# A fused attention and two-MoE kernel: a new order of the first chunks, and the first eight units' second token halves run later, from raw weights

## The chip, the cores and the metric

The kernel runs on one core of one Trainium2 chip. The metric is the device time of one execution in microseconds (us). TensorE (PE), VectorE (DVE), ScalarE (ACT) and GpSimd (POOL) each execute their own instructions in program order; SyncE (SP) issues nearly all DMAs, in order too.

## The reference

Three stages follow each other, in float32.

```python
# attention: 4 batches x 8 heads, 768 tokens, head size 48; per token t
S = (ar + i*ai)/|a| * min(|a|, 0.999) * S + k_t v_t^T     # complex state, decay normalised
y_t = q_t . Re(S)
# MoE 1: 3072 tokens, 384 wide, 4 experts of 1024, dense
out = sum_e p_e * (relu(x @ w1[e]) @ w2[e]),   p = probs / sum(probs)
# MoE 2: 384 -> 2048 -> 384
h = x @ w_in;  out = maximum(0.01 * h, h) @ w_out
```

## The kernel before, in words

**Attention** is cut into 24 chunks of 128 tokens. `elementwise(c)` (L167 to L251) turns one chunk's inputs (`aaqk`, one 768 KB load) into features `ft` by some thirty operations on DVE, ACT and POOL: logarithms and exponentials of the decay, two prefix scans (L202, L207), a phase scan (L219), sine and cosine, and last the products with q and k (L243). `by_head(c)` copies `ft` by six SBUF to SBUF DMAs into `hd`, a layout by head (L261). `products(c)` is TensorE work: `pt` transposes (L279), scores `sc` (L292), the state `pm`/`st`, the output `py`, its transposes `px` (L325), from which ACT and DVE make `xh` and `xl` (L333, L334), the high and low part of the next stage's input.

**MoE 1 and MoE 2** run in units of 128 hidden columns: 32 units for MoE 1 (`u` 0 to 31), 16 for MoE 2, over six groups `g` of 512 tokens. Each product of two float32 numbers is made from high and low parts by three matmuls. A whole unit is `gemm_in` (nine matmuls into `ph`, L442), `hp` on DVE (L447), its split into `hh` on ACT and `hl` on DVE (L459, L460), and `gemm_out` (nine matmuls into `acc`, L471 to L473). In group 0 a weight comes raw from HBM (384 KB, L402), is split by an ACT cast and a POOL subtraction (`split_unit`, L418, L419) and stored as a high and low pair (768 KB, L608); later uses reload that pair (L410). Four raw buffers and seven split buffers are used in turn (`RAWS`, `WTS`).

**The order** is written out by hand. The list `order` (L379) names the units: the first eight units on tokens 0 to 255, the same eight on tokens 256 to 511 (with reloaded pairs), then units 8 to 31 whole. The main loop (L591) runs two units ahead with `gemm_in`. The attention of the first four chunks is partly run before the loop, by the string `PLAN`: each digit runs `elementwise` of that chunk up to its next `yield`, `p`, `q`, `r`, `t` do the same for `products` of chunks 0 to 3, `s` splits one weight half, `n` normalises the probabilities. The rest of the attention is `background()` (L516): its `yield`s are ticks, run between the halves of units at the speed that `pace` gives, so that each group's chunks are done before its units. Within a chunk's 26 ticks, `PSTEPS` says which belong to `products(c)`; the others run `elementwise(c + 1)`. The inputs of chunk c+2 are loaded at the start of chunk c's ticks (L532), ahead of `by_head(c)` in SP's queue. `warm` (L161) puts matmuls without use into TensorE's queue early on.

Of the kernel before, what the change touches and what calls it, by code (L numbers as in the profile page):

```python
# [11 lines left out]
F32 = mybir.dt.float32  # L12
# [8 lines left out]
P = 128  # L21
NT = B * S
DM = H * D
# [11 lines left out]
NHALF = 8  # L35
WARM = 1, 2, 3, 0
# [4 lines left out]
FTK = (1,)  # L41
TPOOL = 6
# [5 lines left out]
DEC = 33.0  # L48
PSTEPS = (1, 3, 5, 8, 10, 13, 16, 18, 21)
ESTEPS = 16  # L50
NSTEPS = ESTEPS + len(PSTEPS)
WAIT = 4
HDG = (1,)
AR_MAX = 1e4
# [7 lines left out]
def fused_kernel(  # L62
# [20 lines left out]
    with ExitStack() as fast:  # L83
# [25 lines left out]
        ones = const.tile([P, P], F32, name="ones")  # L109
        G.memset(ones, 1.0)  # L110
        zero_b = const.tile([P, 1], F32, name="zero_b")
        G.memset(zero_b, 0.0)
# [47 lines left out]

        def warm(x, n):  # L161

            out = ps_acc.tile([P, TG], F32, name="warm", tag="acc0")
            for _ in range(n):
                PE.matmul(out[:, : NG * P], ident, x.rearrange("p g t -> p (g t)"), start=True, stop=True)

        def elementwise(c):  # L167
# [14 lines left out]
            table("natural_log_exp_and_others")  # L182
            act(r, g, AF.Ln)
            act(a, g, AF.Square)
            T = V if c < TPOOL else G
            S = G if c < 2 else T
            S.tensor_tensor(b, en, en, ALU.mult)
            yield
            T.tensor_tensor(a, a, b, ALU.add)
            act(r, r, AF.Exp, scale=-1.0)  # L190
# [4 lines left out]
            act(a, a, AF.Ln)  # L195
            S.tensor_tensor(r, en, r, ALU.mult)
            yield
            act(b, a, AF.Exp, scale=-0.5, bias=ln_b)
            yield
# [8 lines left out]
            G.tensor_tensor(q, q, en, ALU.mult)  # L208
            act(a, b, AF.Exp, scale=-0.5)
            yield  # L210
            table("trig_and_small")
            act(r, r, AF.Arctan)
            V.scalar_tensor_tensor(b, en, -1.0, a, ALU.mult, ALU.mult)
            V.scalar_tensor_tensor(a, b, 2.0, a, ALU.add, ALU.mult)
# [5 lines left out]
            if c >= CPG:  # L220
                yield
# [3 lines left out]
            if c >= CPG:  # L225
                yield
# [11 lines left out]
            act(cs[:, 0], g, AF.Sin, scale=-1.0, bias=pi_b)  # L238
            if c == 1:
                warm(th, WARM[1])  # L240
            yield
            for i, x in ((0, q), (1, k)):
                (G if i and c in FTK else V).tensor_tensor(  # L243
                    ft[:, :, :, i * P : (i + 1) * P], cs,
                    x[:, None].to_broadcast([P, 2, NG, P]), ALU.mult,
                )
                if i or c >= CPG:
                    yield
            feats[c] = (ft, vt)
# [18 lines left out]
        def products(c):  # L268
# [7 lines left out]
            for ri in range(2):  # L276
# [7 lines left out]
                yield  # L284
            if c < 2:
                warm(last_phase[c], WARM[2])
            att = pool.tile([P, H, P], F32, name="att", bufs=1)
            for hh in range(2):
# [58 lines left out]
        stored = []  # L347

        def decode(i):
            u, half = divmod(i, 2)  # L350
# [16 lines left out]
            A.copy(wt[:, 0], wo)  # L367
            G.tensor_tensor(wt[:, 1], wo, wt[:, 0].bitcast(F32), ALU.subtract)
            yield
            load_raw64(i + 3)  # L370
            if stored:
                SP.dma_start(*stored.pop())
            stored.append((ws[NU1 + u][:, half], wt.bitcast(F32)))

# [16 lines left out]
        raws, wts, pbs, hs, x2 = {}, {}, {}, {}, {}  # L391
        seen = set()
        fresh = [u not in seen and not seen.add(u) and u < NU1 for _, u, _ in order]

# [17 lines left out]
        def split_unit(s, part):  # L412
            if s >= len(order) or not fresh[s]:
                return
            if s not in wts:
                wts[s] = p_w.tile([P, 2, 2, DM], F32R, name="wt", bufs=WTS)
            raw, wt = raws[s][:, part], wts[s][:, part]
            A.copy(wt[:, 0], raw)  # L418
            G.tensor_tensor(wt[:, 1], raw, wt[:, 0].bitcast(F32), ALU.subtract)  # L419
            if part:  # L420
                del raws[s]

        def load_pb(s):
            if s >= len(order) or order[s][1] >= NU1 or order[s][1] % 8 or order[s][2][0]:
                return
            g, e = order[s][0], order[s][1] // 8
            pb = p_h.tile([P, TG], F32, name="pb", bufs=2)
            SP.dma_start(pb, pn_d[e : e + 1, g * TG : (g + 1) * TG].to_broadcast([P, TG]))
            pbs[g, e] = pb
# [33 lines left out]
        def gemm_out(s, acc):  # L463
            u, (t0, t1) = order[s][1:]
            first, last = u in (0, NU1) and t0 == 0, u in ends
            wt = wts.pop(s)[:, 1]
            hh, hl = hs.pop(s)
            for dc in range(NG):
                cols = slice(dc * P, (dc + 1) * P)
                out = acc[dc][:, t0:t1]  # L470
                PE.matmul(out, wt[:, 0, cols], hh, start=first, stop=False)  # L471
                PE.matmul(out, wt[:, 1, cols], hh, start=False, stop=False)  # L472
                PE.matmul(out, wt[:, 0, cols], hl, start=False, stop=last)  # L473

# [14 lines left out]
        with tc.manual_schedule():  # L489
# [12 lines left out]
            steps.update(zip("pqrt", (products(c) for c in range(CPG))))  # L502
            splits = iter([(0, 0), (0, 1), (1, 0), (1, 1), (2, 0), (2, 1), (3, 0)])
            for x in PLAN + "0" * 14 + "1" * 14 + "pq" * 8 + "s" * 7:
                if x in steps:
                    next(steps[x], None)
                elif x == "n":
                    normalise_probs()
                    load_pb(0)
                elif x == "s":  # L510
                    for s, part in islice(splits, 1):
                        split_unit(s, part)
                        if part and s < 2:
                            load_unit(s + 5)

            def background():  # L516
                for _ in zipped(steps["2"], steps["3"]):
                    yield
# [26 lines left out]
            def decoding():  # L545
# [5 lines left out]
                yield  # L551
                SP.dma_start(*stored.pop())

            dec = decoding()

            first = max(0, 14 - min(PLAN.count("2"), PLAN.count("3"))) + WAIT + E2 - PLAN.count("r") - PLAN.count("t")
            pace = [(0.0, 0), (KN, first)]
# [33 lines left out]
            for s in range(len(order)):  # L591
# [233 lines left out]
```

## Time and profile before

| | before |
|---|---|
| median of three runs | 1506.38 us (1501.48, 1506.38, 2019.27) |
| profiled execution | 1506.07 us, of which its span 1504.2 us |
| TensorE busy | 1403.8 us, 93% of the span |
| VectorE / ScalarE / GpSimd busy | 57% / 38% / 18% |

A window row gives, for a stretch of the span, each engine's busy time, the granted TensorE clock as a share of 2.4 GHz, and the DMA engines' share and rate. A waits row gives what an engine's line waited for: total, times, longest. A timeline row begins with start and duration and ends with the idle time before it and what ended that, in brackets. "SPq" and "ACTq" are DMAs by the queue that issued them.

### The profile page before, as it was taken

The page shows a single profiled execution, that of the slowest core. Times are in us where ns is not written, and L with a number is a line of the kernel's source. Part 1 is how long each engine was busy: PE and PEld are TensorE (multiplying, and loading weights), DVE is VectorE, ACT ScalarE, POOL GpSimd, SP SyncE. Part 2 cuts the span into 40 slices and gives each one's busy share as a digit, 9 for nine tenths or more (in the row PEclk, how much of TensorE's full clock was granted, in tenths as well). Part 3 has the DMA queues.
Part 4 walks back from the last instruction along what each step waited for, and adds up shares of the span by engine and source line. Part 5 has one row for each costly group of instructions (what it writes and reads, how often), then busy time and mean ns, then how long its engine had stood idle before and what let it go on. Part 6 is the DMA issues. An engine that isn't in the chain of part 4 may idle for free.

```text
span 1504.2 us, 18506 instructions
## 1 busy us (share of the span) xinstructions
PE 1403.8 (93%) x6972; PEld 1177.8 (78%) x6972; DVE 864.8 (57%) x1503; ACT 566.7 (38%) x957; POOL 263.6 (18%) x251
## 2 busy tenths in 40 slices
PE   1888888999899989999999999999999999999997
PEld 0787667888777878878888888888888888888886
DVE  8838566669787878876455555455443333333332
ACT  5535455533444344355333354333242111323232
POOL 5113455311223122121001021001010000100000
PEclk9789989999999999999999999999999999999999
DMA  5498776887788698776776575676565655556562
GB/s 194 53 321 262 243 224 210 246 290 241 236 271 259 248 286 254 264 243 192 236 226 195 195 229 170 232 226 171 178 200 175 218 202 204 193 189 210 190 210 65
DMA packets 91042, 325.48 MB, mean 216 GB/s; under 512 B 10464, under 2 KB 32064, under 8 KB 90944
## 3 DMA queue, kind: packets, MB, share of 16 engines
q1 hardware_dynamic: 88064, 319.24, 66.8%
q10 hardware_dynamic: 2880, 4.98, 1.0%
q8 instruction: 56, 0.92, 0.3%
q14 instruction: 42, 0.34, 0.1%
HBM read 262.72 MB, written 42.52 MB: 203 GB/s over the span
## 4 chain that ended last, share of the span: by engine, by line
PE 60%; DVE 8%; DMA 3%; ACT 2%; issue 2%; POOL 0%; SPq 0%; DVEq 0%; ACTq 0%; POOLq 0%
PE ph L442 27%; PE acc L471 9%; PE acc L473 9%; PE acc L472 9%; DVE hl L460 2%; PE sc L292 1%; PE py L315 1%; PE py L317 1%; DMA vt<-in_v_dram 1%; DVE hp L447 1%; ACT hh L459 1%; DMA ws_scratch<-dw 1%; PE pm L303 1%; DVE ft L243 1%; DMA r<-in_w_dram 1%
## 5 line engine op out<-in xcount | busy, mean ns | idle before, releaser
L442 PE MATMUL ph<-xh,wt 128*128 128x512 f32 (+1 forms) x1200 | 407.5, 396 | 6.9 <-DMA wt<-ws_scratch 6.3
L471 PE MATMUL acc<-hh,wt 128*128 128x512 f32 (+1 forms) x888 | 350.0, 394 | 6.9 <-ACT o L586 6.9
L473 PE MATMUL acc<-hl,wt 128*128 128x512 f32 (+1 forms) x888 | 341.9, 385 | 0.0
L472 PE MATMUL acc<-hh,wt 128*128 128x512 f32 (+1 forms) x888 | 341.2, 384 | 0.0
L459 ACT CAST hh<-hp 128x512 fp32r<-128x512 f32 (+1 forms) x296 | 180.6, 610 | 402.1 <-DVE hp L447 315.4
L460 DVE TENSOR_TENSOR hl<-hp,hh 128x512 fp32r<-128x512 f32 (+1 forms) x296 | 213.5, 721 | 183.6 <-ACT hh L459 183.1
L442 PEld LDWEIGHTS ph<-xh,wt 128*128 128x128 f32 x1200 | 231.4, 195 | 51.8 <-DMA wt<-ws_scratch 7.4
L447 DVE SCALAR_TENSOR_TENSOR hp<-ph,pb 128x512 f32<-128x512 f32 (+1 forms) x200 | 133.4, 667 | 199.9 <-PE ph L442 199.8
L442 PE MATMUL ph<-xl,wt 128*128 128x512 f32 (+1 forms) x600 | 234.5, 391 | 1.1 <-DVE xl L334 1.1
L442 PE MATMUL ph<-x2h,wt 128*128 128x512 f32 x576 | 198.0, 398 | 0.0
L471 PEld LDWEIGHTS acc<-hh,wt 128*128 128x128 f32 x888 | 167.5, 189 | 38.2 <-ACT o L586 7.6
L473 PEld LDWEIGHTS acc<-hl,wt 128*128 128x128 f32 x888 | 167.1, 188 | 34.1
L472 PEld LDWEIGHTS acc<-hh,wt 128*128 128x128 f32 x888 | 167.7, 189 | 31.0
L450 DVE SCALAR_TENSOR_TENSOR hp<-hp 128x512 f32<-128x512 f32 x96 | 72.3, 753 | 171.7 <-ACT hp L449 171.7
L442 PEld LDWEIGHTS ph<-xl,wt 128*128 128x128 f32 x600 | 117.4, 196 | 22.0 <-DVE xl L334 1.6
L442 PEld LDWEIGHTS ph<-x2h,wt 128*128 128x128 f32 x576 | 108.7, 189 | 25.2
L449 ACT COPY hp<-ph 128x512 f32<-128x512 f32 x96 | 56.3, 586 | 168.0 <-PE ph L442 168.0
L442 PE MATMUL ph<-x2l,wt 128*128 128x512 f32 x288 | 114.5, 397 | 0.0
L292 PE MATMUL sc<-hd 96*128 96x128 f32 x384 | 58.3, 302 | 35.8 <-DMA hd<-ft 26.7
L292 PEld LDWEIGHTS sc<-hd 96*128 96x128 f32 x384 | 55.7, 215 | 42.8 <-issue 22.7
L419 POOL TENSOR_TENSOR wt<-raw,wt 128x384 fp32r<-128x384 f32 x64 | 71.9, 1144 | 57.2 <-ACT wt L418 56.9
L208 POOL TENSOR_TENSOR aaqk<-aaqk,ge 128x384 f32<-128x384 f32 x24 | 26.5, 1103 | 252.1 <-DVE ge L207 252.1
(94 smaller groups left out, 1467.2 us busy)
## 6 DMA issues: line engine op xcount, KB each, us to landing
wt<-ws_scratch SPq DMA_DIRECT2D x264, 768.0 KB, 4.8
ws_scratch<-wt SPq DMA_DIRECT2D x32, 768.0 KB, 8.1
hd<-ft SPq DMA_DIRECT2D x142, 128.5 KB, 7.2
aaqk<-in_attn_dram SPq DMA_DIRECT2D x22, 768.0 KB, 5.8
raw<-in_w_dram SPq DMA_DIRECT2D x32, 384.0 KB, 4.1
r<-in_w_dram SPq DMA_DIRECT2D x32, 384.0 KB, 3.8
ws_scratch<-dw SPq DMA_DIRECT2D x32, 384.0 KB, 4.2
pb<-pn_scratch SPq DMA_DIRECT2D x24, 256.0 KB, 6.5
```

Source lines behind the costliest of these rows:

```text
L208: G.tensor_tensor(q, q, en, ALU.mult)
L292: PE.matmul(sc[:, j], hd[:, h, P : 2 * P], hd[:, h, :P], start=True, stop=True)
L419: G.tensor_tensor(wt[:, 1], raw, wt[:, 0].bitcast(F32), ALU.subtract)
L442: PE.matmul(ph[:, : t1 - t0], wt[:, wi, cols], x[kc][:, t0:t1], start=n == 0, stop=n == 3 * NG - 1)
L447: V.scalar_tensor_tensor(hp, ph, 0.0, pbs[g, u // 8][:, t0:t1], ALU.max, ALU.mult)
L449: A.copy(hp, ph)
L450: V.scalar_tensor_tensor(hp, hp, 0.01, hp, ALU.mult, ALU.max)
L459: A.copy(hh, hp)
L460: V.tensor_tensor(hl, hp, hh.bitcast(F32), ALU.subtract)
L471: PE.matmul(out, wt[:, 0, cols], hh, start=first, stop=False)
L472: PE.matmul(out, wt[:, 1, cols], hh, start=False, stop=False)
L473: PE.matmul(out, wt[:, 0, cols], hl, start=False, stop=last)
```

## The change

Four things are done.

1. **Units of group 0.** After the first eight halves come units 8 to 15 whole, then, alternating, a whole unit (16 to 23) and a second half (0 to 7), then 24 to 31. Second halves load the raw weight again and split it again; the pair is stored only at that second time, and the eight reloads are gone. Unit 8's `gemm_out` runs in two column halves.
2. **Before the loop.** `warm` is gone. `PLAN` runs chunks 0 and 1 first and gives chunks 2 and 3 fewer steps; what is left of them runs in the ticks. Six weight halves are cast on ACT (`cast_early`), their low part is made by TensorE (identity times raw minus identity times high) and copied by ACT (`rest_early`), instead of by POOL. Chunks 0 and 1 issue three of their six `hd` DMAs each from ACT. Within `elementwise`, `Square` stands before `Ln`, and more `yield`s cut it finer; `ft` with k of chunk 1 is on DVE, not on POOL.
3. **Ticks.** Three more steps of `elementwise(c + 1)` stand between `by_head(c)` (step 1) and the scores (step 12 in place of 8), and `load_chunk(c + 2)` moves to step 9, behind `by_head`.
4. **Decoding of MoE 2's weights.** A store is issued one part later, and the next raw load after a `yield`.

The core of the diff:

```diff
-PLAN = "0100100111100n10s1s0s100s1s0s00110s22113p2q1332p322q32p2p3q2p3q3q2q3p23pq2pq223333"
+PLAN = (
+    "0101001010101011" "01ss0000mm" "00sss11mm000" "1111ppsm23111qq"
+    "23232n3pp23p2ppqq3q23qqpq23m"
+)
-PSTEPS = (1, 3, 5, 8, 10, 13, 16, 18, 21)
-ESTEPS = 16
+PSTEPS = (1, 3, 5, 12, 14, 17, 20, 22, 24)
+ESTEPS = 17
+LOADSTEP = 9
...
-                (G if i and c in FTK else V).tensor_tensor(
+                V.tensor_tensor(
...
-                    (A if c in HDG and i == ri else SP).dma_start(hd[row : row + DG], ft[:, ri, i])
+                    (A if c < 2 and (i == ri or i == 2 - ri) else SP).dma_start(hd[row : row + DG], ft[:, ri, i])
...
-        order = [(0, u, half) for half in halves for u in range(NHALF)] + first_stage(0)[NHALF:]
+        order = [(0, u, halves[0]) for u in range(NHALF)] + first_stage(0)[NHALF : 2 * NHALF]
+        for u in range(NHALF):
+            order += [(0, 2 * NHALF + u, whole), (0, u, halves[1])]
+        order += first_stage(0)[3 * NHALF :]
...
-        fresh = [u not in seen and not seen.add(u) and u < NU1 for _, u, _ in order]
+        fresh = [g == 0 and u < NU1 for g, u, _ in order]
...
+        def cast_early(s, part):
...
+            A.copy(wts[s][:, part, 0], raws[s][:, part])
+            early_cast.append((s, part))
+
+        def rest_early():
...
+            rest = ps_h.tile([P, TG], F32, name="ph")[:, :DM]
+            PE.matmul(rest, ident, raw, start=True, stop=False)
+            PE.matmul(rest, minus, wt[:, 0].bitcast(F32), start=False, stop=True)
+            A.copy(wt[:, 1], rest)
...
                 for c in range(CPG, NCHUNK):
-                    if c + 2 < NCHUNK:
-                        load_chunk(c + 2)
                     todo = products(c)
                     ahead = elementwise(c + 1) if c + 1 < NCHUNK else iter(())
                     for k in range(NSTEPS):
+                        if k == LOADSTEP and c + 2 < NCHUNK:
+                            load_chunk(c + 2)
                         next(todo if k in PSTEPS else ahead, None)
...
-                if fresh[s]:
+                if fresh[s] and t1 == TG:
                     SP.dma_start(ws[u], wts[s].bitcast(F32))
```

**SP's queue around the `hd` DMAs of chunk 4**, the first chunk whose attention runs wholly in the ticks (`raw`: a weight, `aaqk` and `vt`: a later chunk's inputs). Before:

```order
L402 DMA raw<-in_w_dram 128x768 x2
L148 DMA aaqk<-in_attn_dram 128x1536
L152 DMA vt<-in_v_dram 128x384
L261 DMA hd<-ft 16x8x257 x6
L402 DMA raw<-in_w_dram 128x768 x4
```

Now:

```order
L394 DMA raw<-in_w_dram 128x768
L448 DMA pb<-pn_scratch 128x512
L251 DMA hd<-ft 16x8x257 x6
L638 DMA ws_scratch<-wt 128x1536
L394 DMA raw<-in_w_dram 128x768
L638 DMA ws_scratch<-wt 128x1536
L150 DMA aaqk<-in_attn_dram 128x1536
L154 DMA vt<-in_v_dram 128x384
```

The two input loads stood right ahead of the six `hd` DMAs; they now stand some rows behind them.

**VectorE where the loop begins** (`xl`: end of chunks 0 and 1; `hp`, `hl`: the first units; the lines below L260 without these: chunks 2 and 3). Before:

```order
L228 TENSOR_SCALAR ge<-th 128x384
L334 TENSOR_TENSOR xl<-px,xh 128x3x128 x2
L243 TENSOR_TENSOR ft<-cs,aaqk 128x6x128 x2
L234 COPY ft<-ge 128x6
L243 TENSOR_TENSOR ft<-cs,aaqk 128x6x128 x2
L447 SCALAR_TENSOR_TENSOR hp<-ph,pb 128x256
L460 TENSOR_TENSOR hl<-hp,hh 128x256
```

Now:

```order
L320 TENSOR_TENSOR xl<-px,xh 128x3x128 x2
L203 SCALAR_TENSOR_TENSOR ge<-ta,ones 128x128 x6
L467 SCALAR_TENSOR_TENSOR hp<-ph,pb_340 128x256
L480 TENSOR_TENSOR hl<-hp,hh 128x256
L467 SCALAR_TENSOR_TENSOR hp<-ph,pb_340 128x256
L480 TENSOR_TENSOR hl<-hp,hh 128x256
L467 SCALAR_TENSOR_TENSOR hp<-ph,pb_340 128x256
L210 SCALAR_TENSOR_TENSOR tb<-ge 128x384
L211 SCALAR_TENSOR_TENSOR ta<-tb,ge 128x384
L216 SCALAR_TENSOR_TENSOR th<-ones,th,tr 128x128 x3
```

Before, the features of chunks 2 and 3 were finished ahead of the first unit's `hp`. Now the first units' `hp` and `hl` stand among the steps of these chunks, whose `ft` comes later.

**TensorE at the scores of chunk 2.** Before, chunk 2's `pt` and the first four scores stood together, with the fifth unit's `gemm_in` (`ph`) behind them:

```order
L473 MATMUL acc_552<-hl,wt 128x256
L279 MATMUL pt<-ident,ft 128x128 x3
L292 MATMUL sc<-hd 128x128 x4
L442 MATMUL ph<-xh,wt 128x256
```

Now, with the sixth unit's `gemm_in` between `pt` and `sc`:

```order
L498 MATMUL acc_508<-hl,wt 128x256
L269 MATMUL pt<-ident,ft 128x128 x6
L462 MATMUL ph<-xh,wt 128x256
L462 MATMUL ph<-xl,wt 128x256
L462 MATMUL ph<-xh,wt 128x256 x2
...
L462 MATMUL ph<-xh,wt 128x256
L280 MATMUL sc<-hd 128x128 x8
L289 MATMUL pm<-vt,kt 96x48 x8
L496 MATMUL acc_506<-hh,wt 128x256
```

Ahead of chunk 2's first scores stood four half units' `gemm_in` and two `gemm_out`; now six and three. By the `px` of chunk 3 it is eight and five in both.

## Rows read from the trace of the kernel before

**Rows 1.** The page: span, and each engine's busy time, share and instructions.

```profile
span 1504.2 us, 18506 instructions
PE 1403.8 (93%) x6972; PEld 1177.8 (78%) x6972; DVE 864.8 (57%) x1503; ACT 566.7 (38%) x957; POOL 263.6 (18%) x251
```

**Rows 2.** Windows: stretch, its length, busy per engine, granted clock, DMA share, GB/s.

```profile
0.00:71.00 71.00, 31.66 (x164) 24.71 (x165) 62.63 (x118) 38.34 (x62) 25.93 (x32) 0.87 0.46 123
66.00:108.00 42.00, 36.58 (x260) 35.88 (x261) 16.85 (x32) 11.79 (x25) 9.05 (x9) 0.79 0.94 255
108.00:300.00 192.00, 165.94 (x911) 142.89 (x911) 124.14 (x217) 97.99 (x175) 82.26 (x75) 0.93 0.78 241
300.00:700.00 400.00, 378.49 (x1898) 316.90 (x1897) 319.97 (x589) 168.06 (x285) 92.23 (x85) 0.97 0.78 256
```

**Rows 3.** Waits of PE, from 108 to 300 us: us in total, times, longest.

```profile
PE sc L292 <- DMA hd<-ft: 21.4, 4, 7.1
PE ph L442 <- DMA wt<-ws_scratch: 3.2, 3, 1.3
PE sc L292 <- ACT tb L119: 1.5, 1, 1.5
```

**Rows 4.** Waits of PE, from 300 to 700 us.

```profile
PE acc L471 <- ACT o L586: 6.9, 2, 4.2
PE sc L292 <- ACT hh L459: 6.3, 1, 6.3
PE sc L292 <- DMA hd<-ft: 4.5, 2, 2.7
```

**Rows 5.** Timeline of the prologue: start, duration, engine, line, operation.

```profile
65.92 0.58 PE L442 MATMUL ph<-xh,wt 128*128 128x256 f32 x1 [0.57 <-ACT xh L333]
67.51 1.82 DVE L243 TENSOR_TENSOR ft<-cs,aaqk 128x768 f32<-128x768 f32 x2
69.39 7.75 SPq L261 DMA_DIRECT2D hd<-ft  x12
78.40 1.13 PE L292 MATMUL sc<-hd 96*128 96x128 f32 x8 [0.99 <-ACT kt L280]
108.06 0.50 PE L325 MATMUL px<-ident,y 128*128 128x128 f32 x3
71.05 0.42 DVE L447 SCALAR_TENSOR_TENSOR hp<-ph,pb 128x256 f32<-128x256 f32 x1
39.55 1.44 ACTq L261 DMA_DIRECT2D hd<-ft  x2
41.03 0.84 ACT L280 COPY kt<-pt 128x384 f32<-128x384 f32 x1 [3.69 <-DVE ta L189]
```

**Rows 6.** Timeline: the phase scans of two chunks, of one shape.

```profile
21.66 3.34 DVE L219 TENSOR_TENSOR_SCAN th<-ones,tr 128x128 f32<-128x128 f32 x3
58.11 1.22 DVE L219 TENSOR_TENSOR_SCAN th<-ones,th,tr 128x128 f32<-128x128 f32 x3
```

**Rows 7.** The page: the weight subtraction on POOL, all 64 of them.

```profile
L419 POOL TENSOR_TENSOR wt<-raw,wt 128x384 fp32r<-128x384 f32 x64 | 71.9, 1144 | 57.2 <-ACT wt L418 56.9
```

**Rows 8.** Timeline: chunk 6 from its features to its scores.

```profile
204.43 3.51 DVE L243 TENSOR_TENSOR ft<-cs,aaqk 128x768 f32<-128x768 f32 x2
207.96 0.33 SPq L148 DMA_DIRECT2D aaqk<-in_attn_dram  x1
209.88 5.10 SPq L261 DMA_DIRECT2D hd<-ft  x6
221.81 2.05 PE L292 MATMUL sc<-hd 96*128 96x128 f32 x8 [7.15 <-DMA hd<-ft]
```

**Rows 9.** The chain of waits at 394 us: a whole unit's `gemm_in`.

```profile
393.88 2.05 PE ph L442 x9
```

**Rows 10.** DMA from 100 to 116 us, with the queues full.

```profile
DMA packets 1232, 6.17 MB, mean 386 GB/s; under 512 B 134, under 2 KB 262, under 8 KB 1230
```

**Rows 11.** The page, DMA issues: a pair's store, its size, us to landing.

```profile
ws_scratch<-wt SPq DMA_DIRECT2D x32, 768.0 KB, 8.1
```

More of the change, by code (lines that the diff above doesn't have):

```diff
@@ L2 @@
 from contextlib import ExitStack
-from itertools import islice
 import concourse.bass as bass
@@ L40 @@
 PT = 32
-FTK = (1,)
 TPOOL = 6
@@ L159, in table @@
                 tables[0] = name
[L161 to L165, printed above, removed]
         def elementwise(c):
@@ L182, in elementwise @@
             table("natural_log_exp_and_others")
-            act(r, g, AF.Ln)
-            act(a, g, AF.Square)
             T = V if c < TPOOL else G
             S = G if c < 2 else T
+            act(a, g, AF.Square)
+            act(r, g, AF.Ln)
             S.tensor_tensor(b, en, en, ALU.mult)
@@ L212, in elementwise @@
             act(r, r, AF.Arctan)
-            V.scalar_tensor_tensor(b, en, -1.0, a, ALU.mult, ALU.mult)
-            V.scalar_tensor_tensor(a, b, 2.0, a, ALU.add, ALU.mult)
+            yield
+            V.scalar_tensor_tensor(b, en, -1.0, g, ALU.mult, ALU.mult)
+            V.scalar_tensor_tensor(a, b, 2.0, g, ALU.add, ALU.mult)
             G.tensor_tensor(k, k, a, ALU.mult)
@@ L347, in fused_kernel, with store_decoded @@
         stored = []
+        def store_decoded(left):
+            while len(stored) > left:
+                SP.dma_start(*stored.pop(0))
         def decode(i):
@@ L368, in decode @@
             G.tensor_tensor(wt[:, 1], wo, wt[:, 0].bitcast(F32), ALU.subtract)
+            stored.append((ws[NU1 + u][:, half], wt.bitcast(F32)))
             yield
[L370 to L373, printed above, removed]
+            store_decoded(1)
+            if i:
+                load_raw64(i + 2)
         whole, halves = (0, TG), ((0, TG // 2), (TG // 2, TG))
@@ L412, in split_unit @@
         def split_unit(s, part):
-            if s >= len(order) or not fresh[s]:
+            if s >= len(order) or not fresh[s] or (s, part) in early_done:
                 return
@@ L421, in split_unit @@
                 del raws[s]
+        early_cast, early_done = [], set()
+        def cast_early(s, part):
+            if s not in wts:
+                wts[s] = p_w.tile([P, 2, 2, DM], F32R, name="wt", bufs=WTS)
+            A.copy(wts[s][:, part, 0], raws[s][:, part])
+            early_cast.append((s, part))
+        def rest_early():
+            if not early_cast:
+                return
+            s, part = early_cast.pop(0)
+            raw, wt = raws[s][:, part], wts[s][:, part]
+            rest = ps_h.tile([P, TG], F32, name="ph")[:, :DM]
+            PE.matmul(rest, ident, raw, start=True, stop=False)
+            PE.matmul(rest, minus, wt[:, 0].bitcast(F32), start=False, stop=True)
+            A.copy(wt[:, 1], rest)
+            early_done.add((s, part))
+            if part:
+                del raws[s]
         def load_pb(s):
-            if s >= len(order) or order[s][1] >= NU1 or order[s][1] % 8 or order[s][2][0]:
+            if s >= len(order) or order[s][1] >= NU1 or order[s][1] % 8:
                 return
             g, e = order[s][0], order[s][1] // 8
-            pb = p_h.tile([P, TG], F32, name="pb", bufs=2)
+            if (g, e) == (0, 0):
+                if order[s][2][0]:
+                    return
+                pb = pools["raw"].tile([P, TG], F32, name="pb0")
+            else:
+                pb = p_h.tile([P, TG], F32, name="pb", bufs=2)
             SP.dma_start(pb, pn_d[e : e + 1, g * TG : (g + 1) * TG].to_broadcast([P, TG]))
@@ L467, in gemm_out @@
             hh, hl = hs.pop(s)
+            parts = [(t0, t1)]
+            if (order[s][0], u) == (0, NHALF):
+                parts = list(halves)
             for dc in range(NG):
                 cols = slice(dc * P, (dc + 1) * P)
[L470 to L473, printed above, removed]
+                for a0, a1 in parts:
+                    out = acc[dc][:, a0:a1]
+                    hhp, hlp = hh[:, a0 - t0 : a1 - t0], hl[:, a0 - t0 : a1 - t0]
+                    PE.matmul(out, wt[:, 0, cols], hhp, start=first, stop=False)
+                    PE.matmul(out, wt[:, 1, cols], hhp, start=False, stop=False)
+                    PE.matmul(out, wt[:, 0, cols], hlp, start=False, stop=last)
         def zipped(*gens):
@@ L502, in fused_kernel @@
             steps.update(zip("pqrt", (products(c) for c in range(CPG))))
-            splits = iter([(0, 0), (0, 1), (1, 0), (1, 1), (2, 0), (2, 1), (3, 0)])
-            for x in PLAN + "0" * 14 + "1" * 14 + "pq" * 8 + "s" * 7:
+            early_halves = iter([(s, part) for s in range(6) for part in (0, 1)][: PLAN.count("s")])
+            for x in PLAN + "m" * 8:
                 if x in steps:
@@ L510, in fused_kernel @@
                 elif x == "s":
[L511 to L514, printed above, removed]
+                    cast_early(*next(early_halves))
+                elif x == "m":
+                    rest_early()
+            for s in (5, 6):
+                load_unit(s)
+            split_unit(3, 0)
             def background():
+                for _ in range(2):
+                    next(steps["2"])
+                    yield
                 for _ in zipped(steps["2"], steps["3"]):
@@ L551, in decoding @@
                 yield
-                SP.dma_start(*stored.pop())
+                store_decoded(0)
             dec = decoding()
-            first = max(0, 14 - min(PLAN.count("2"), PLAN.count("3"))) + WAIT + E2 - PLAN.count("r") - PLAN.count("t")
+            first = 2 + max(0, ESTEPS + 1 - min(PLAN.count("2"), PLAN.count("3"))) + WAIT + E2 - PLAN.count("r") - PLAN.count("t")
             pace = [(0.0, 0), (KN, first)]
```

32 lines of the change are left out of this document (10 added, 22 removed).

## The prediction, before the change was run

> **What bounds the kernel now.** I read the page first. TensorE is busy 1403.8 of 1504.2 us, no other engine above 57% [rows 1]: the time is TensorE's work plus its idle stretches plus what a lowered clock costs. The profiled execution took 1506.07 us, 1.9 us more than its span and 0.3 below the median of the three runs (1506.38), so the sum below is made against the span, and the result is also that against the median.
>
> Then I read the windows, to see where TensorE is idle or slow [rows 2]. Before the first `gemm_in` at 65.92 [rows 5] it has little to do: VectorE is busy 62.63 of the first 71 us and sets the start. From 66 to 108 us TensorE is idle 42.0 - 36.58 = 5.4 us and its clock is 0.79 of 2.4 GHz, which costs 42 x 0.21 = 8.8 us. From 108 to 300 us it is idle 192 - 165.94 = 26.1 us, and the clock of 0.93 costs 192 x 0.07 = 13.4. From 300 to 700 us it is idle 21.5 us, and the clock of 0.97 costs 400 x 0.03 = 12. After 700 us little is left to gain: 1403.8 less some 609 of busy time before leaves 795 of 804 us.
>
> Last the waits. From 108 to 300 us the scores wait 21.4 us for the `hd` DMAs, and 1.5 us more that are put down to ACT but stand at the same instruction: 22.9 us of the 26.1. Reloaded weights cost 3.2 [rows 3]. From 300 to 700 us the scores wait 4.5 and, in the same way, 6.3 us, so 10.8 of 21.5; the rest is mostly the evacuation of a group [rows 4]. One chunk shows how the wait comes about [rows 8]: chunk 6's `ft` ends at 204.43 + 3.51 = 207.94; SP then issues `aaqk` and `vt` first, the `hd` DMAs come from 209.88 on, and the scores start at 221.81 after 7.15 us of waiting. TensorE's instructions are in order, so the units behind stand too.
>
> The low clock seems to hang on these gaps: of the three windows, the one from 300 to 700 us has the smallest idle share (5% against 13 and 14) and the highest clock [rows 2]. So I price a pause as paid a second time through the clock.
>
> **The change, part by part.**
>
> *A. The prologue, up to `px` of chunk 3 (108.06 before [rows 5]): +4.5 us.* The first `gemm_in` itself comes earlier, by my estimate at 57 to 60 us, since it no longer stands behind all of chunks 2 and 3 on VectorE. But TensorE soon meets the scores of chunk 2 in its order, and they need `ft` of chunk 2, which now comes late on VectorE. Its end, before 67.51 + 1.82 = 69.3, I work out from the end of the same VectorE work, 71.1:
> - less 1.8, the `ft` of chunk 3, which does not count;
> - less 5.1: POOL's weight subtractions are gone from there, seven at 1.144 us = 8.0 us [rows 7]; beside POOL's work a phase scan takes 3.34 us, alone 1.22 [rows 6], so in 8.0 us VectorE loses up to 8.0 x (1 - 1.22/3.34) = 5.1 (0 to 6);
> - plus 0.9, half of an `ft` of 1.82, for k of chunk 1, which POOL made;
> - plus 3.0 for four `hp` and three `hl`, which now stand ahead, seven at about 0.42 [rows 5];
> - plus 4: ACT issues three `hd` DMAs for each of chunks 0 and 1 (1.44 for two, so 2.2 for three) and two `kt` copies (2 x 0.84) [rows 5] ahead of the `Square` of chunk 2 for which VectorE waits (0 to 6);
> - plus 6: the `hp` ahead of it need `ph`, nine matmuls at 0.58 = 5.2 us each at the low clock [rows 5]; VectorE waits for one of them and a bit, having other work beside the rest (0 to 10).
>
> That gives 78.1. From `ft` to scores it took 78.40 - 69.33 = 9.1 us, so the scores start at 87. What TensorE has to do from the first `gemm_in` to `px` of chunk 3 is 42 - 5.4 - 8.8 = 27.8 us at full clock. Of this, six `gemm_in` and three `gemm_out` stand ahead of the scores, each half of 2.05 [rows 9], together 9.2, with 0.6 of transposes; 18.0 remain. Behind a pause of some 15 us the clock will be low for a while, +5 (the whole window lost 8.8 before), and +2.5 for its waits, about half of the 5.4. So `px` of chunk 3 is at 87 + 25.5 = 112.5, 4.5 later. Bounds from the terms' own: -4 to +11. That six low parts are now made on TensorE costs nothing by itself: it is idle more than half of the first 71 us [rows 2]; without that cover it would be twelve matmuls of 384 columns, against 0.58 for 256 [rows 5] some 0.9 each, 10 us.
>
> *B. No reloads in group 0: -3.2* [rows 3].
>
> *C. `hd` waits from 108 to 300 us: -16.9, and clock -7.4.* Between `by_head` and the scores now lie eleven ticks instead of seven. A group-0 unit gets (4 x 27 + 17 of ticks)/27 = 4.6 of them, before (4 x 26 + 16)/27 = 4.4; so the scores come 11/4.6 - 7/4.4 = 0.8 of a unit later. A unit is 2 x 2.05 = 4.1 us [rows 9]: 3.3 us. And `hd` no longer stands behind `aaqk` and `vt`: 1.9 us from the end of `ft` to the issue [rows 8], and 0.98 MB of load on the same DMA engines, at 386 GB/s [rows 10] 2.5 us; I take 1 to 3. Of the four large waits (up to 7.1) 3.3 + 1 to 3.3 + 3 each goes as far as it lasts; I leave 6 in all of 22.9. The clock's 13.4 goes down with it; I leave 6. Bounds: half (-12) to all (-36) of both.
>
> *D. From 300 to 700 us: -9, and clock -4.* Here a unit has fewer ticks and the same four ticks are 1.1 to 1.7 units, 4.5 to 6.8 us; the 10.8 us of waits go down to about 2. Of the clock's 12 I take a third, since the evacuation's gaps stay. Bounds together -5 to -18.
>
> *E. DMA in the alternation: +6.* For each pair of a whole unit and a second half, two raw loads and two stores are 2 x (384 + 768 KB) = 2.36 MB, at 386 GB/s [rows 10] 6.1 us. A chunk's `aaqk`, `vt` and `hd` per six units add about 2.4. That is 8.5 us against 4.1 + 2.05 of units and some 2 of attention on TensorE: even, with no slack. Whatever is late is then not caught up; I take 6 (0 to 15).
>
> *The rest: 0.* Unit 8's nine additional matmuls split work of the same columns; the decode edits move SP issues by a part, behind raw loads that are used three parts later; pb and constants are outside the path.
>
> Sum: 4.5 - 3.2 - 16.9 - 7.4 - 9 - 4 + 6 = -30.0, span 1474, time 1476.
>
> *A rule and the row beside it.* The rows give 386 GB/s with the DMA engines full [rows 10]. The Trainium skill, DMA: Bandwidth & Descriptors, section "Where 436 GB/s comes from", says that traffic between HBM and SBUF is held by the HBM side at about 358 GB/s for a core. By that, a pair's 2.36 MB would take 6.6 us in place of 6.1, with a chunk's loads 0.7 more a pair, and by an estimate from that E would be larger by 8 x 0.7 = 6 us, the time 1482. The row shows more than that rate over 16 us, so the row decides.
>
> **The rivals.**
>
> *R1, the prologue is really ahead.* If VectorE's waits for `Square` and `ph` (4 + 6) are covered by its other work, `ft` of chunk 2 ends at about 68, the scores come at 77 with half the stall, and `px` of chunk 3 at 77 + 18 + 2.5 + 3 = 100.5, so A is about -7 and the time 1464. For: VectorE has some 8 us of idle time already, which can hold such waits. Against: its order now has `hp` of units ahead of `ft`.
>
> *R2, the `hd` wait comes back.* Sixteen more half splits on POOL (16 x 1.144 = 18 us [rows 7]) fall into a stretch where an `ft` already takes 3.51 instead of 1.82 [rows 8, 5], and the six `hd` DMAs must go through full queues. If half of C and D (37.3) is eaten, the time is 1495. For: both `ft` and landing are longest there. Against: POOL is busy less than half of that window [rows 2].
>
> *R3, slower than before: the ring of split buffers.* There are seven, and each of the sixteen steps of the alternation holds its own until its store has landed. A buffer is taken again seven units on and is filled four ahead, so a store has about three steps, 9 to 12 us, to land; the median is 8.1 [rows 11]. If a full queue makes it 16, three steps take 16 us: 16/3 x 16 = 85 in place of 63 to 66 us of work; +20, +6 in E withdrawn, and +18 in clock and lost gains of C in the same stretch: about 1508. It decides from a landing of about 12 us on, and is slower than before from 16. For: no slack in E. Against: the median.
>
> *R4, the waits just move.* If the scores wait for something else at once (vt late, since its load now stands behind), two thirds of C and D (37.3) are lost: 1476 + 25 = 1501. Against: the loads are for two chunks on.
>
> **How the numbers follow.** Forecast 0.45 (its own range 1466 to 1487), R1 0.2, R2 0.2, R3 0.09, R4 0.06. The predicted time is the forecast's, 1476. The range 1455 to 1502 holds R1 with A at its lower bound, the forecast and R2, and R4, and leaves out R3 and the extremes, less than 0.2. Two per cent, about what a measurement of this kernel can tell from no change, is 1476.3 here, in the middle of the forecast. Half of the forecast and all of R1 are below it: 0.43 faster. Over 1536 is only an R3 with landings far over 16 us and a prologue at its upper bound: 0.05. The rest, 0.52, is within 2%.
>
> **What would show it.** A: the first `gemm_in` before 61 us, but the scores of chunk 2 behind 84, with a clock of 0.5 after them; R1 if these stand before 79. B: no wait for reloaded weights before 300 us. C: waits for `hd` from 108 to 300 us of 6, and a clock of 0.96 or more; R2 if they are over 12. D: 2 to 3 us of such waits after 300. E: `ph` or the splits waiting for raw weights, 6 us from about 150 to 220 us; R3 if `ph` waits for a split that itself waits for a store. The prediction would be wrong above all if VectorE, not the DMAs, makes `ft` late everywhere: then four ticks more move only the wait.

## The result

| | before | changed |
|---|---|---|
| median | 1505.77 us (4 runs) | 1487.64 us (1485.56 to 1489.82, 4 runs) |
| profiled execution, span | 1506.07, 1504.2 us | 1485.91, 1484.2 us |
| ratio | | 0.989, 95% interval 0.986 to 0.992 |
| TensorE busy | 1403.8 us, 93% | 1405.6 us, 95% |

The kernel is 18 us faster, 1.1%: inside the range of 1455 to 1502, less than the 30 us of the sum. The prediction had given 0.52 to a change of less than 2%. One of the four runs of before took 2019.27 us, and the ratio leaves it out. Windows of the changed kernel, columns as in [rows 2]:

```profile
0.00:66.00 66.00, 37.57 (x152) 30.62 (x153) 41.32 (x87) 31.20 (x56) 10.17 (x20) 0.75 0.49 125
66.00:108.00 42.00, 25.59 (x163) 24.18 (x161) 27.23 (x49) 13.11 (x28) 14.11 (x13) 0.74 0.57 114
108.00:300.00 192.00, 176.28 (x1031) 153.60 (x1032) 148.40 (x226) 105.82 (x197) 105.45 (x93) 0.96 0.82 263
300.00:700.00 400.00, 391.19 (x1975) 327.96 (x1974) 332.48 (x602) 178.39 (x301) 96.22 (x86) 0.99 0.79 266
```

From 66 to 108 us TensorE is now idle 16.4 us (5.4 before), from 108 to 300 us 15.7 (26.1), from 300 to 700 us 8.8 (21.5); the clock of the last two is higher. Its waits from 66 to 108 us:

```profile
PE pt L269 <- DVE ft L234: 9.4, 1, 9.4
PE sc L280 <- DMA hd<-ft: 5.5, 1, 5.5
```

From 108 to 300 us, answering to [rows 3]:

```profile
PE pt L269 <- DVE ft L234: 8.9, 1, 8.9
PE sc L280 <- DMA hd<-ft: 4.8, 2, 2.9
PE px L311 <- ACT y L307: 1.7, 3, 0.6
```

From 300 to 700 us, answering to [rows 4], these are all:

```profile
PE acc L496 <- ACT o L616: 5.2, 2, 3.3
PE px L311 <- ACT y L307: 3.5, 2, 2.4
```

The waits for `hd` shrank as forecast. New is a wait of 8.9 us for chunk 4's features, and before it the prologue is late. TensorE's timeline there, answering to [rows 5]:

```profile
66.79 0.57 PE L462 MATMUL ph<-xh,wt 128*128 128x256 f32 x1
86.99 1.51 PE L269 MATMUL pt<-ident,ft 128*128 128x128 f32 x6 [9.37 <-DVE ft L234]
95.87 3.75 PE L280 MATMUL sc<-hd 96*128 96x128 f32 x16 [5.46 <-DMA hd<-ft]
122.05 0.55 PE L311 MATMUL px<-ident,y 128*128 128x128 f32 x3 [0.57 <-ACT y L307]
151.49 0.87 PE L269 MATMUL pt<-ident,ft 128*128 128x128 f32 x3 [8.87 <-DVE ft L234]
```

The end of group 0 is where ScalarE starts the first copies of `acc`, before and now:

```profile
294.42 1.56 ACT L586 COPY o<-acc 128x512 f32<-128x512 f32 x3
293.20 1.56 ACT L616 COPY o<-acc 128x512 f32<-128x512 f32 x3
```

So the difference, by three marks: `px` of chunk 3 is 14.0 us later (122.05 against 108.06); the end of group 0 is at 293.2 against 294.4, so 15.2 us are won in between; the last matmul ends at 1475.0 against 1495.0, another 18.8.

### The profile page after: what moved, and what is told of

Same layout as the page of the kernel before. It is cut to its first block, busy times and chain, and to the rows that moved or that the text cites. A ratio compares the mean times of both kernels' runs of the same rounds, so it can differ in the third digit from the quotient of the medians.

```text
span 1484.2 us, 18601 instructions
## 1 busy us (share of the span) xinstructions
PE 1405.6 (95%) x6987; PEld 1181.1 (80%) x6987; DVE 875.5 (59%) x1504; ACT 570.4 (38%) x977; POOL 283.9 (19%) x260
## 4 chain that ended last, share of the span: by engine, by line
PE 57%; DVE 2%; ACT 0%; issue 0%; DVEq 0%; ACTq 0%
PE ph L462 26%; PE acc L496 9%; PE acc L498 9%; PE acc L497 9%; PE sc L280 1%; PE py L301 1%; PE py L303 1%; PE pm L289 1%; PE pt L269 0%; DVE hl L480 0%; DVE hp L467 0%; PE px L311 0%; DVE d L349 0%; ACT hh L479 0%; DVE d L354 0%
## 5 line engine op out<-in xcount | busy, mean ns | idle before, releaser
L462 PE MATMUL ph<-xh,wt 128*128 128x512 f32 (+1 forms) x1200 | 399.9, 389 | 0.0
L480 DVE TENSOR_TENSOR hl<-hp,hh 128x512 fp32r<-128x512 f32 (+1 forms) x296 | 217.1, 734 | 151.6 <-ACT hh L479 150.2
L462 PEld LDWEIGHTS ph<-xh,wt 128*128 128x128 f32 x1200 | 226.8, 191 | 43.0 <-POOL wt L411 0.2
L462 PE MATMUL ph<-xl,wt 128*128 128x512 f32 (+1 forms) x600 | 231.1, 385 | 0.0
L411 POOL TENSOR_TENSOR wt<-raw,wt 128x384 fp32r<-128x384 f32 x74 | 84.5, 1164 | 70.8 <-ACT wt L410 50.2
L655 POOL TENSOR_TENSOR x2l<-o,x2h 128x512 fp32r<-128x512 f32 x18 | 25.1, 1422 | 256.4 <-ACT x2h L654 256.4
L301 PE MATMUL py<-vt,att 128*128 128x48 f32 x384 | 71.0, 279 | 0.1
```

What stands on the lines that cost most here:

```text
L301: PE.matmul(py[:, h], att[:, h], vt[:, h * D : (h + 1) * D], start=True, stop=first)
L462: PE.matmul(ph[:, : t1 - t0], wt[:, wi, cols], x[kc][:, t0:t1], start=n == 0, stop=n == 3 * NG - 1)
L480: V.tensor_tensor(hl, hp, hh.bitcast(F32), ALU.subtract)
```

## Experiments

Where two runs were not measured side by side, their difference is also given by the ratios to the kernel before, which was measured beside each; 0.001 of a ratio is 1.5 us.

On part 3: by `PSTEPS` it is four more steps of `elementwise(c + 1)`, not three, that stand between `by_head(c)` and the scores (eight in place of four). In e5 to e8 and e10 to e12 the changed `elementwise`, with its finer cut and `Square` ahead of `Ln`, serves the chunks from 4 on; the list of the change has it under part 2, here it counts with part 3.

| run | what it is | median us | ratio (95%) |
|---|---|---|---|
| changed | parts 1 to 4 | 1487.6 | 0.989 (0.986 to 0.992) |
| e1 | 1, 4, a cruder 3 | 1482.9 | 0.988 (0.984 to 0.992) |
| e2 | the cruder 3 alone | 1483.4 | 0.987 (0.984 to 0.991) |
| e3 | 1 alone | 1510.1 | 1.0045 (1.003 to 1.006) |
| e4 | changed, with `warm` | 1493.1 | 0.993 (0.991 to 0.996) |
| e5 | 1, 3, 4: part 2 undone | 1473.4 | 0.978 (0.976 to 0.981) |
| e6 | e5 with a gap | 1472.8 | 0.979 (0.976 to 0.982) |
| e7 | 3, 4: parts 1 and 2 undone | 1470.9 | 0.978 (0.975 to 0.981) |
| e8 | e5, POOL relieved | 1471.2 | 0.977 (0.974 to 0.980) |
| e9 | changed, `PLAN` altered | 1483.6 | 0.985 (0.982 to 0.988) |
| e10 | e7, old load step | 1482.4 | 0.985 (0.981 to 0.989) |
| e11 | e7, old distance | 1483.8 | 0.984 (0.981 to 0.987) |
| e12 | 3 alone | 1473.9 | 0.978 (0.974 to 0.982) |

**e1 and e2: parts of the change on the kernel before.** Both have this in place of part 3, with `load_chunk` called at step 9 and `elementwise` as before; e1 adds the new order and the new decoding.

```diff
-PSTEPS = (1, 3, 5, 8, 10, 13, 16, 18, 21)
+PSTEPS = (1, 3, 5, 11, 13, 16, 19, 21, 23)
+LOADSTEP = 9
...
```

Expected of e1: 

> The changed kernel with the prologue of before: parts 1 and 4 as changed, of part 3 the later load and scores three ticks later (step 11 of 25), part 2 undone. Theory 1, the new prologue alone makes both losses (px of chunk 3 14.0 us later, 8.9 us of waiting for the features of chunk 4): px of chunk 3 at about 108 us, no wait for chunk 4's features over 1 us, 1460 to 1470 us. Theory 2, the wait for chunk 4 comes from VectorE beside more POOL splits or from the ticks: it stays at 6 to 9 us and the time is 1472 to 1477. Theory 3, later stages had the slack for a late start: 1484 to 1490.

Expected of e2: 

> Before, with the later load and scores three ticks later and nothing else. Theory 1, the distance between hd and scores made the waits: 22.9 us of waits for hd between 108 and 300 us go to 6 or less, 10.8 between 300 and 700 us to 2 or less, and the clock there rises to 0.97 or more: 1464 to 1472 us. Rival, the features are late on VectorE and the wait only moves: waits at pt in their place, 1495 to 1506.

e2 took 1483.4 us: the ticks alone bring as much as the whole change. Its waits for `hd` are 5.9 us from 108 to 300 us and none from 300 to 700, as theory 1 had it. Its time is above theory 1's, and the waits from 300 to 700 us show what came in their place:

```profile
PE px L326 <- ACT y L322: 7.5, 3, 2.9
PE acc L472 <- ACT o L587: 6.1, 2, 3.3
PE pm L304 <- DVE att L294: 4.3, 2, 2.2
```

In place of `hd`, steps that follow the scores wait for ScalarE and VectorE; that these are then busy with a coarse step of `elementwise(c + 1)` is my reading. The changed kernel, with the finer cut, has 3.5 us at `px` and none at `pm`; e12, whose order and prologue are those of e2, has 0.8 and 1.5.

e1 took 1482.9 us and fits none of its three theories. `px` of chunk 3 is at 100.6, as theory 1 had it, but the wait at `pt` of chunk 4 is still 8.8 us, as theory 2 had it: that wait does not come from the prologue. e1 differs from the changed kernel in the prologue and also in the step table and the cut of `elementwise`; e5 below parts them.

**e3: the order of units alone.** The change of `order`, `fresh`, the store and `pb` is put on the kernel before.

> Before, with the units of group 0 in the new order, second halves from raw weights, old ticks and old prologue. Theory 1, the order is worth the reloads alone: the 3.2 us of reload waits gone, hd waits between 108 and 300 us still 15 us or more, 1498 to 1506 us. Rival, the queues are relieved by the order and that is what shortened the hd waits: these under 10 us, 1480 to 1492.

It is 0.45% slower than the kernel before, with an interval clear of zero, which neither theory had. TensorE's waits from 108 to 300 us:

```profile
PE sc L292 <- DMA hd<-ft: 27.1, 4, 7.0
PE pt L279 <- DVE ft L243: 8.8, 1, 8.8
```

The reload waits are gone, the waits for `hd` are not smaller, and the wait for chunk 4's features is there: it belongs to the order. `px` of chunk 3 comes at 102.4, 5.7 us sooner than before: the order brings this mark forward by itself, and loses it again by the end of group 0, at 301.6 (294.4 before).

**e4: the warm-ups again.**

```diff
             last_phase[c] = th
+            if c == 0:
+                warm(th, WARM[0])
             yield
```

and likewise at the other two places of before.

> The changed kernel with the warm-up matmuls of before put back at the same steps of chunks 0 and 1. Theory A, the prologue is late because TensorE runs chunks 0 and 1 at half its clock (30 to 66 us) and VectorE stands for it: their scores and outputs take about half as long, the first gemm_in comes at 58 to 62 instead of 66.8 us, px of chunk 3 at 112 to 117, 1478 to 1483 us. Theory B, VectorE's and ScalarE's own order sets the prologue: first gemm_in within 2 us of 66.8, 1485 to 1490.

Both theories missed: it is 5.5 us slower than the changed kernel (ratio 0.993 against 0.989). The first 66 us:

```profile
0.00:66.00 66.00, 34.20 (x163) 25.52 (x164) 40.41 (x85) 29.46 (x52) 10.17 (x20) 0.91 0.50 125
```

The granted clock is 0.91 in place of 0.75, and yet the first `gemm_in` comes at 69.3 us, 2.5 later. The warm-ups stand in TensorE's queue ahead of scores that are on the path:

```profile
38.77 2.10 PE L168 MATMUL warm<-th,ident 128*128 128x384 f32 x6
41.34 2.02 PE L293 MATMUL sc<-hd 96*128 96x128 f32 x16 [0.47 <-DMA hd<-ft]
55.11 3.61 PE L168 MATMUL warm<-th,ident 128*128 128x384 f32 x6
58.56 1.61 PE L293 MATMUL sc<-hd 96*128 96x128 f32 x13
```

What the clock is worth can still be read here, from the first scores of chunk 1 to its `px`. In the changed kernel and in e4 these are

```profile
50.60 3.75 PE L280 MATMUL sc<-hd 96*128 96x128 f32 x16
63.45 1.67 PE L311 MATMUL px<-ident,y 128*128 128x128 f32 x6
```

```profile
65.83 1.67 PE L324 MATMUL px<-ident,y 128*128 128x128 f32 x6
```

that is 12.9 us with a clock of 0.50 from 50 to 66 us, and 7.3 us in e4 (from 58.56), with 0.93 from 58 to 66. So theory A is right about the products, but they begin 8.0 us later, with the warm-ups right ahead of them. From 66 to 108 us the clock of e4 is 0.62, below the 0.74 of the changed kernel. The removal of the warm-ups by itself is not what makes the new prologue late.

**e5: part 2 alone undone.** The prologue of before, all else as changed; the finer `elementwise` serves chunks from 4 on.

> The changed kernel with part 2 alone undone: from chunk 4 on its steps are those of the changed kernel (scores at step 12 of 26), before the loop all is as before. Theory 1, the new prologue costs what it is late at the end of group 0: px of chunk 3 at about 100 us and the end of group 0 at 275 instead of 293, carried to the end: 1468 to 1472 us. Rival, the 18 us are given back in groups 1 and 2, as in the first experiment (1482.9), because the later stages have slack for a late start: 1480 to 1488.

1473.4 us, near theory 1: the new prologue costs some 14 us (by the ratios 16). `px` of chunk 3 is at 101.1, 21.0 us before the changed kernel's, and the end of group 0 at 274.8, 18.4 us before it; 5.5 of these are given back by the last matmul. So the 14.0 us at `px` of chunk 3 in the result are two things: some 21 lost by the new prologue and some 7 won by the order. Its waits from 108 to 300 us still hold the one at `pt`:

```profile
PE pt L360 <- DVE ft L325: 7.0, 1, 7.0
PE sc L373 <- DMA hd<-ft: 6.3, 3, 3.5
PE px L406 <- ACT y L402: 2.7, 1, 2.7
```

From e1 to e5 only the step table (scores at step 12 in place of 11) and `elementwise` differ: 9.5 us by the medians, 14 by the ratios.

**e6: a gap ahead of chunk 4's `pt`.**

```diff
                 for _ in elementwise_new(CPG):
                     yield
+                for _ in range(GAP):
+                    yield
...
```

The eight ticks are also added to `pace`.

> As the one with part 2 alone undone, and eight empty ticks between the features of chunk 4 and its hd and pt. If the wait of 8.8 us at pt of chunk 4 is only TensorE arriving too early: the wait is under 2 us, and the time 7 to 11 us below that one's. If VectorE is behind by itself from then on, the wait comes at a later chunk and the time is within 4 us of that one's.

The wait is gone and the time the same (1472.8 against 1473.4). The waits for `hd` from 108 to 300 us grew from 6.3 to 8.9, and a wait of 2.9 for `hh` is new; the end of group 0 is at 274.9, as in e5. The second theory holds: moving TensorE's arrival only moves the wait.

**e7: the old order too.**

> Before, with the changed ticks and steps from chunk 4 on and the changed decoding; order and prologue of before. It differs from the one with part 2 alone undone by the order alone. Theory 1: no wait over 2 us for the features of chunk 4, but reload waits of 2 to 3 us and px of chunk 3 at 108: within 3 us of that one. Rival, the order is worth more or less than that in the queues: over 5 us apart.

1470.9 us, as theory 1 had it: with the new ticks, the order is worth nothing that can be told apart (0.978 both). e7 has the lowest median of all, 2.2% below before and 1.1% below the changed kernel, but e5, e6 and e12 have the same ratio within their intervals. From 108 to 300 us its waits are

```profile
PE sc L373 <- DMA hd<-ft: 5.9, 2, 4.5
PE ph L527 <- DMA wt<-ws_scratch: 1.9, 3, 0.9
```

**e8: POOL without subtractions beside chunk 4.**

```diff
-            G.tensor_tensor(wt[:, 1], raw, wt[:, 0].bitcast(F32), ALU.subtract)
+            if 8 <= s < 18:
+                A.copy(wt[:, 1], raw)
+            else:
+                G.tensor_tensor(wt[:, 1], raw, wt[:, 0].bitcast(F32), ALU.subtract)
```

This kernel leaves out the low parts of ten units' weights, so it serves only as a measurement.

> As the one with part 2 alone undone, but for the units 8 to 17 of the list the low part of the weight is not computed: ACT makes a second copy in its place, so that POOL has no weight subtraction while chunk 4's features are made. If POOL beside VectorE makes these features late: from the first operation to the end of ft 27.5 us become 19 to 21, a scan of three at most 1.5 us and the two ft at most 2.0, and the wait of 8.8 us at pt of chunk 4 falls under 2. If it is the larger hp and hl of whole units: 25 us or more and a wait over 6.

Windows from the first operation on chunk 4 to the end of its `ft`, for e7 (old order), e5 and e8:

```profile
109.50:128.60 19.10, 17.19 (x138) 16.59 (x139) 17.63 (x42) 11.37 (x23) 4.31 (x4) 1.00 0.97 377
```

```profile
103.30:129.30 26.00, 19.10 (x102) 16.19 (x101) 22.98 (x38) 14.93 (x28) 13.52 (x12) 0.96 0.54 175
```

```profile
103.50:127.20 23.70, 18.55 (x98) 15.69 (x98) 17.93 (x38) 18.65 (x38) 2.13 (x2) 0.95 0.55 190
```

In between the two theories. Without POOL's subtractions VectorE is busy 17.9 us in place of 23.0, as in the old order: POOL beside it costs 5 us. The larger `hp` and `hl` are a small part: together they take 6.4 us in e5, 6.2 in e8 and 5.3 in e7. But VectorE's idle time grows from 3.0 to 5.8 us, and the wait at `pt` is still 5.3 us (7.0 in e5). VectorE's largest wait in these windows, in e5 and in e8:

```profile
DVE hl L552 <- ACT hh L551: 1.5, 2, 0.8
```

```profile
DVE hl L555 <- ACT hh L554: 4.5, 3, 3.1
```

The idle time that e8 adds is waiting for ScalarE, which e8 itself made busier, 18.7 us in place of 14.9. So its 5.3 us do not measure what would be left without POOL; that the second copies cause them is likely but was not tested apart.

Between e7 and e5 the account is plainer. In e5 these features are begun 6.2 us sooner than in e7 and are done 0.7 us later, so what the order wins is lost there. The changed kernel shows the same beside the kernel before:

```profile
109.90:128.80 18.90, 15.74 (x126) 15.12 (x127) 16.96 (x41) 10.30 (x19) 3.04 (x3) 1.00 0.95 353
```

```profile
123.90:151.40 27.50, 18.71 (x98) 15.66 (x98) 25.51 (x37) 15.29 (x27) 15.12 (x12) 0.89 0.36 116
```

The stretch is 8.6 us longer, and VectorE's busy time is 8.6 us longer: here it is not standing. `hp` and `hl` take 1.6 us of that (7.4 in place of 5.8); the rest is slower steps of the chunk itself, with 15.1 us of POOL work in the stretch in place of 3.0.

**e9: five more steps of chunk 2 ahead.**

```diff
-    "23232n3pp23p2ppqq3q23qqpq23m"
+    "23232n3pp23p2ppqq3q23qq2222322pq3m"
```

> The changed kernel with one string changed: in PLAN five more steps of chunk 2 and one of chunk 3 stand ahead of the last steps of chunks 0 and 1. In the changed kernel VectorE waits 6.9 us for xh of chunk 1 with the scans of chunk 2 behind it in its order. Theory 1, VectorE's order makes the prologue late: this wait falls under 2 us, ft of chunk 2 ends at 70 to 76 us instead of 86.8, px of chunk 3 comes at 106 to 114 instead of 122, 1474 to 1481 us. Rival, TensorE's half clock or the low parts made there do: px of chunk 3 at 118 or later, 1485 to 1489.

In between again: 1483.6 us, 4 less than the changed kernel (by the ratios 6). `px` of chunk 3 is at 119.3. In the changed kernel VectorE waited here, ahead of the scans of chunk 2:

```profile
64.86 0.56 DVE L320 TENSOR_TENSOR xl<-px,xh 128x384 fp32r<-128x384 f32 x1 [6.86 <-ACT xh L319]
66.15 2.77 DVE L203 TENSOR_TENSOR_SCAN ge<-ta,ones 128x128 f32<-128x128 f32 x6
```

With the scan ahead of `xl`, VectorE runs it at once and then stands behind ScalarE:

```profile
56.79 1.04 DVE L203 TENSOR_TENSOR_SCAN ge<-ta,ones 128x128 f32<-128x128 f32 x3
63.58 0.56 DVE L210 SCALAR_TENSOR_TENSOR tb<-ge 128x384 f32<-128x384 f32 x1 [5.74 <-ACT ge L121]
```

ScalarE's exponential for chunk 2 stands behind the copy of `y` of chunk 1, which waits for TensorE's `py`. So not one order but two, VectorE's and ScalarE's, hold chunk 2 behind chunk 1's products.

Two more things stand in e9's trace. Its `ft` of chunk 2 ends at 83.8 us, 3.1 sooner, but the scores start only 1.1 sooner, at 94.74, after a wait that the changed kernel does not have:

```profile
PE sc L280 <- ACT kt L270: 10.0, 1, 10.0
```

And ScalarE loads a function table four times between 63 and 79 us, at 1.28 us each, where the changed kernel does so once: its steps now alternate between two sets of functions. What either costs e9 was not tested apart.

**e10 and e11: the two halves of part 3, undone on e7.**

```diff
-LOADSTEP = 9
+LOADSTEP = 0
```

```diff
-PSTEPS = (1, 3, 5, 12, 14, 17, 20, 22, 24)
+PSTEPS = (1, 3, 5, 8, 10, 13, 17, 20, 23)
```

Expected of e10: 

> As the one with the old order and prologue and the changed ticks (1470.9), but a later chunk's inputs are loaded ahead of hd in SP's queue again (step 0). If the queue's order is worth what was forecast, 1 to 3 us of each large wait: 6 us of hd waits between 108 and 300 us become 10 to 16, 1474 to 1482 us. If only the distance to the scores counts: within 2 us.

Expected of e11: 

> As the one with the old order and prologue and the changed ticks (1470.9), but the scores at step 8 after by_head at step 1 again; the inputs stay behind hd. If the distance is the larger part: hd waits of 12 us or more between 108 and 300 us and 6 or more between 300 and 700, the clock of both back to 0.95 or less and 0.98 or less, 1482 to 1496 us. If the queue's order alone was it: within 3 us.

Each costs: 11.6 us for the load (by the ratios 11), 12.9 for the distance (10). e11's waits for the scores from 108 to 300 us are 13.5 us, as expected, and its clock is 0.93 there; from 300 to 700 us, where I had expected 6 us or more and a clock of 0.98 or less, the scores wait 2.8 and the clock is 0.99, but `acc` waits 9.8 us for `o`, 3.4 in e7. The edit also moves the steps behind the scores a little. From 108 to 300 us:

```profile
PE sc L373 <- DMA hd<-ft: 9.6, 2, 5.3
PE sc L373 <- ACT wt L503: 3.3, 1, 3.3
PE ph L527 <- DMA wt<-ws_scratch: 2.3, 1, 2.3
PE sc L373 <- ACT hh L544: 0.6, 1, 0.6
```

e10's from 108 to 300 us:

```profile
PE sc L373 <- DMA hd<-ft: 6.2, 2, 3.1
PE ph L527 <- DMA wt<-ws_scratch: 3.4, 4, 1.4
PE sc L373 <- ACT wt L503: 2.7, 1, 2.7
```

That is 8.9 at the scores (6.2 and 2.7), below the 10 to 16 expected. Part of e10's loss lies elsewhere: 3.0 us of reload waits from 300 to 700 us, where e7 has none, and a clock of 0.98 there in place of 0.99.

**e12: part 3 alone,** that is e7 with the decoding of before.

> Before with part 3 alone: the one with the old order and prologue and the changed ticks (1470.9), with the decoding of MoE 2's weights as before. Forecast, decoding costs nothing in either form: within 3 us of 1470.9. Rival, SP waiting for a decoded weight held back the transfers behind it between 300 and 700 us: 1475 to 1482, with more than 10.8 us of idle TensorE between 300 and 700 us.

1473.9 us (four runs, 1469.2 to 1478.2), ratio 0.978 as e7: between the two forms of decoding nothing can be told apart, as forecast. TensorE is idle 11.3 us from 300 to 700 us, a little over the rival's 10.8, but none of its waits there is for a weight. The list of the change has this part wrong: by the code the store keeps its part and goes ahead of the load, and it is the raw load that comes one part later.

From e2 to e12, as from e1 to e5, only the step table and `elementwise` differ: 9.6 us by the medians, 15 by the ratios.

## Why the prediction was right and wrong

The direction held and the time lies in the range, but the gain is 18 us by the medians and 20.0 by the spans, against which the sum of 30.0 was made. By the three marks, A came out 9.5 us worse than forecast, B, C and E together 6.3 us worse, and D 5.8 us better. That an error in one stage was partly paid for by another is luck.

*A, the prologue: +4.5 forecast, +14.0 measured, outside its bounds.* The step that failed is the sum for the end of chunk 2's `ft`: 78.1 us forecast, 86.8 measured. Its work was right: 71.1 less the 8.4 us that VectorE is idle up to there, then -1.8 - 5.1 + 0.9 + 3.0, is 59.7 us, and VectorE is busy 60.9 up to 86.84. Its waits were not: VectorE is idle 25.9 us up to there, 17.5 more than before, where the sum had 4 and 6. Of its waits from 0 to 87 us, these tell which:

```profile
DVE xl L320 <- ACT xh L319: 7.1, 2, 6.9
DVE ta L185 <- ACT ta L121: 5.8, 2, 5.3
DVE att L281 <- PE sc L280: 4.2, 2, 3.1
```

The wait for `Square` (`ta`) came about as forecast: 5.8 us, where it was 2.2 before. The 6 us for `ph` did not come: `hp` waits nowhere in this stretch. They were also misread, since the matmuls of [rows 5] overlap: in the low clock before, three of them start within 0.64 us, so nine take 1.9 and not 5.2. In their place VectorE waits for the products of chunks 0 and 1, by way of `xl` and `att`, while TensorE has a clock of 0.50, its lower level of 1.2 GHz, from 40 to 66 us. The step "having other work beside the rest" was wrong: in order, the other work stands behind the wait, and when it is put ahead (e9), ScalarE's order holds it.

The first `gemm_in` was to come at 57 to 60 us and came at 66.79: I took VectorE's busy time for what sets the start. VectorE is now busy 41.3 of the first 66 us (57.7 in e5), and it is TensorE that is busy without a gap from 50 to 66 us, at half its clock, mostly with chunk 1's products. A higher clock shortens these, but bought with warm-ups it does not help (e4). The last of the low parts, put at nothing, stand between `px` of chunk 1 and this `gemm_in` and cost about 1 us (`xh` of chunk 1 is done at 65.64). From `ft` to scores it took 9.0 us (9.1 assumed), and from the scores to `px` 26.2 (25.5). That the order alone brings `px` of chunk 3 forward by 6 to 7 us (e3, e5) was in no term; without it A would have been some 21 us.

*B, no reloads: -3.2, right in itself;* the waits are gone. *E, DMA in the alternation: +6, wrong.* TensorE does not wait for a raw weight or a store from 108 to 700 us, so the limit that the prediction takes from the Trainium skill, DMA: Bandwidth & Descriptors, section "Where 436 GB/s comes from", and that would have made E larger, has no wait here to act on. The order's price is one I had under R2: POOL's subtractions beside VectorE's features, at chunk 4 and not in the alternation (e8). e3 puts the order at +7 us with the old ticks; with the new ones it is level (e5, e7).

*C, waits for `hd` from 108 to 300 us: 6 us forecast, 4.8 measured, and 0.6 more for `kt` at the same place.* The step held. The clock was to leave 6 us of loss, and leaves 192 x 0.04 = 7.7. But 8.9 us of the gain went into chunk 4's features. Between `px` of chunk 3 and the end of group 0, B, C and E forecast -21.5; it was -15.2.

*D, after 300 us: -13 forecast, -18.8 measured.* The waits for `hd` went from 10.8 to none. Idle time from 300 to 700 us fell by 12.7 us and the clock's loss from 12 to 4: I had left two thirds of it. Not foreseen was that the finer cut of `elementwise`, with the scores one step later, is worth another 10 to 15 us (e1 against e5, e2 against e12); the two were not parted.

*Part 4 at nothing* held (e12); the other edits that were put at nothing were not undone by themselves. Of the rivals, R2 named the mechanism of the new wait but not its place; R1 was the reverse of what happened, R3 and R4 did not occur.

In all: part 3 gains some 33 us, part 1 is about level beside it, part 2 takes 14 to 16 back.

## What to carry to other kernels

A busy share tells what an engine must do, not when: before a step of one chunk is put behind another chunk's products, look at what each engine in order will wait for there, and count that wait in full. To shorten a wait for a DMA, give it distance and take other transfers out of its way; here each was worth about ten us. Where several edits come together, undo them one at a time: the best version here had half of them.

## What was not expected

- VectorE's share of chunk 4's features took 23.0 us busy with twelve POOL operations beside it and 17.9 with two (e5, e8). The Trainium skill, SBUF — State Buffer, section "SBUF: two separate sides", has a VectorE operation with two inputs in SBUF and a GpSimd operation that reads SBUF lock each other out of a shared pair of ports for a whole instruction. The rows agree that VectorE pays, 5 us for some 11 us of POOL work; that it pays at the port, no run here shows.
- Warm-ups raised the granted clock of the first 66 us from 0.75 to 0.91 and made the kernel 5.5 us slower.
- Taking away a wait of 7 us by a gap (e6) changed nothing in the time.
